# Fewer transfers for values and sketches, another token layout for keys, and a new order of steps in a fused attention and expert kernel

## The chip, the cores and the metric

The kernel runs on one core of a Trainium2 chip. A core has a matrix engine (TensorE, "PE" in the profile; its weight loads are listed as "PEld"), a vector engine (VectorE, "DVE"), a scalar engine (ScalarE, "ACT"), GpSimd ("POOL") and a sync engine (SyncE, "SP") that issues most transfers. Sixteen DMA engines move data between device memory and the on-chip SBUF; matrix products land in PSUM, in banks of 512 float32 columns. Each engine runs its own instructions in order and waits for others through semaphores. The metric is the time of one execution on the device in microseconds; lower is better.

## The reference

A polynomial-sketch attention feeds an expert layer with a rational activation. Shapes: 4 batches, 4 heads, 1088 tokens, 32 features per head, sketches of size 8; the expert layer has 4352 tokens, width 128 and 2048 hidden units.

```python
def phi(x):
    a = np.einsum('rd,bhsd->bhsr', S1, x)
    b = np.einsum('rd,bhsd->bhsr', S2, x)
    return np.einsum('bhsi,bhsj->bhsij', a, b).reshape(*x.shape[:-1], r * r)
q_p, k_p = (phi(q), phi(k))
kv = np.einsum('bhsf,bhsd->bhfd', k_p, v)
z = np.sum(k_p, axis=2)
num = np.einsum('bhsf,bhfd->bhsd', q_p, kv)
den = np.einsum('bhsf,bhf->bhs', q_p, z)[..., None] + 1e-06
x = num / den                       # heads side by side: 4352 x 128
h = x @ w_in
P = a[0] + a[1] * h + a[2] * h**2 + a[3] * h**3
Q = 1.0 + np.abs(b[0]) * np.abs(h) + np.abs(b[1]) * h**2
out = (P / (Q + 1e-06)) @ w_out
```

The sum over tokens in kv and z does not depend on the order in which a batch's key tokens are laid out, as long as keys and values agree.

## The kernel before

The program is one list of steps, ORDER, written out by hand; a loop at the end of the kernel walks it and emits each step's instructions. There is no scheduler: the place of a step in the list sets its place in the queue of every engine that it uses, and only semaphores hold an instruction back. A step's name has its kind, its batch or unit, and its part; a last ".a" or ".d" puts it on ScalarE or VectorE.

- K steps, batch by batch: T0 to T2 transpose the keys on VectorE (L266, L270), s0 and s1 sketch them on TensorE (L276), c0 and c1 copy one sketch out of PSUM (L242 or L244), f0 and f1 form the 64 features (L288), p0 and p1 multiply them with the values into two PSUM banks (L304), k0 and k1 copy the result into `kvz`.
- Q steps, for a batch's queries in three or four cuts: T transposes (L332), sk sketches, c copies. The first two cuts of batch 0 form the features straight from PSUM (L349, L385). The other eleven, the "spread" ones, write their sketch to a scratch tile `sk_d` in device memory (L365) and read it back (step d), once with each row repeated 8 times (`a_all`, L370) and twice with a block of 8 rows repeated (`b_all`, L373); f multiplies the two (L381). Then p (L392), pl, r and x divide, b transposes back (L420), and kk copies into the ring `xT`.
- The expert layer runs over 22 units (token range, 4 to 16 of the 16 hidden blocks): H is the hidden product in float32 (L471), E moves it to SBUF as bfloat16 on ScalarE, U, W, Y, V, S, G are element-wise passes on VectorE, P is one that either engine can do (L496 on VectorE, L499 on ScalarE), L and X a logarithm and an exponential on ScalarE, Or, Os, Og the three output products (L530), ST and OUT the transpose (L537) and the store (L548).
- F steps fetch a batch's k, v or q; I0 to I3 load `w_in`, the second part of the first queries, the coefficients, and `w_out` (into the tile `ln`); w0 to w5 scale `w_out` into three bfloat16 copies. Zn is n products of a zero tile (L182) that keep TensorE running.

Transfers. Nearly all are issued by SP, in the order of ORDER. The program gives transfers eight completion semaphores in turn, over SP and ACT together; an issue waits until the transfer that last had its semaphore has landed, and everything behind it on SP waits too. The key tile, the query tile and the value tile each have one buffer, so that a fetch also waits for the last reader of the batch before. In the program before, 1088 = 34 x 32 tokens are split so that partition g of a head holds tokens 34g to 34g + 33; a key load is one transfer of 128 rows of 4352 bytes. The values come in four transfers of 32 partitions x 4 heads x 1024 bytes and two of 32 x 4 x 128 bytes. A sketch write is two transfers of 64 rows. The first 512 columns of the first queries are issued by ACT.

Of the kernel before, what the change touches and what calls it, by code (L numbers as in the profile page):

```python
# [30 lines left out]
I0 SS0 K0.T0 K0.T1 Z10 K0.s0 K0.T2 F1.k I1 I2 I3 Q0.0.T K0.s1 K0.c0.a Q0.1.T K0.f0 K0.c1.d Z3 Q0.0.sk K0.f1 K0.p0  # L31
Q0.0.c.d Q0.1.sk Q0.0.f K0.p1 F1.v Q0.1.c.d Q0.1.f K0.k1.a K0.k0.a K1.T0 Z5 Q0.0.p K1.T1 Q0.1.p Q0.2.T Q0.0.pl.a
Q0.0.r K1.T2 Q0.0.x Q0.2.sk Q0.1.pl.a Q0.3.T K1.s0 Q0.2.c.a Q0.1.r Q0.1.x Q0.2.d Q0.0.b K1.c0.d K1.s1 Q0.0.kk.a
K1.f0 H0.0 K1.c1.a K1.f1 w3.a H1.0 AB0 w0.d E0.0 w4.d w5.a U0.0 Q0.3.sk w2.d H2.0 E1.0 W0.0 Q0.3.c.d P0.0.a Y0.0
F1.q Q0.1.b w1.d H2.1 E2.0 U1.0 Q0.1.kk.d L0.0 W1.0 V0.0 K1.p0 E2.1 Y1.0 Q0.3.d K1.p1 Q0.2.f X0.0 U2.0 P1.0.a S0.0
Q0.2.p W2.0 K1.k0.a G0.0 K1.k1.a Or0.0 Q0.2.pl.a Os0.0 L1.0 Q0.2.r Q1.0.T Og0.0 Q0.2.x Q1.0.sk F2.k.v X1.0 Q1.1.T
Q0.2.b Y2.0 Q1.1.sk Q0.2.kk.a Or1.0 Q1.0.c.a H3.0 Q1.2.T L2.0 V1.0 S1.0 H3.1 P2.0.d E3.0 G1.0 X2.0 V2.0 F2.q H3.2
Q0.3.f Q1.0.d E3.1 S2.0 Q0.3.p E3.2 Q1.1.c.d H3.3 G2.0 Q0.3.pl.a P3.0.a K2.T0 H4.0 Q0.3.r Q2.0.T E3.3 Q0.3.x K2.T1
P3.1.a K2.s0 U3.0 H4.1 K2.T2 W3.0 K2.c0.a E4.0 K2.f0 Os2.0 E4.1 Q0.3.b Y3.0 H4.2 Q0.3.kk.a P4.0.a Q1.1.d H4.3
Q1.0.f E4.2 V3.0 L3.0 Q1.0.p Q1.2.sk Q2.0.sk Q1.0.pl.d E4.3 Q1.0.r Q2.1.T Or2.0 Q1.0.x X3.0 U4.0 Os1.0 Q1.0.b  # L40
Og1.0 P4.1.d Og2.0 Q1.0.kk.a L3.1 Q2.2.T H5.0 ST2 F3.q W4.0 OUT2 Q1.2.c.a H5.1 V4.0 X3.1 K2.s1 Q1.2.d E5.0 Q1.1.f
Or3.0 Q2.0.c.a Y4.0 E5.1 H5.2 K2.c1.a P5.0.a K2.f1 Q2.1.sk Q1.1.p L4.0 S3.0 Or3.1 H5.3 Q1.1.pl.a E5.2 Q1.1.r
Q3.0.T X4.0 G3.0 H6.0 E5.3 Or4.0 Q1.1.x E6.0 U5.0 Og3.0 Q2.0.d P5.1.a Q1.2.f H6.1 W5.0 L4.1 V5.0 H6.2 E6.1 X4.1
Q1.2.p Y5.0 H6.3 E6.2 S4.0 Q1.2.pl.a Q2.1.c.a Or4.1 L5.0 Q1.1.b Os3.0 Q1.2.r G4.0 Q1.1.kk.a E6.3 H7.0 X5.0 Q2.1.d
Q2.0.f H7.1 U6.0 P6.0.a Q1.2.x Og4.0 W6.0 E7.0 P6.1.d L5.1 Q1.2.b Y6.0 H7.2 E7.1 Os4.0 X5.1 V6.0 H7.3 E7.2 ST4
Q1.2.kk.a P7.0.d OUT4 L6.0 H8.0 S5.0 K2.p0 E7.3 X6.0 Q2.1.f H8.1 U7.0 P7.1.a Q2.2.sk G5.0 K2.p1 Or5.0 Q2.2.c.a
F3.k.v K2.k0.a W7.0 K2.k1.a Or5.1 L6.1 Os5.0 Q3.1.T V7.0 E8.0 Or6.0 X6.1 Q3.0.sk Y7.0 H8.2 Q2.2.d E8.1 Q2.0.p S6.0
Q3.0.c.a E8.2 H8.3 P8.0.a Q3.2.T G6.0 Q2.1.p E8.3 Og5.0 Q2.0.pl.a L7.0 U8.0 Or6.1 Q2.0.r P8.1.a W8.0 Og6.0 Q2.0.x
K3.T0 X7.0 Y8.0 Q2.0.b K3.s0 Q3.0.d Os6.0 Q2.1.pl.a Q2.0.kk.a L7.1 Q2.2.f Q2.1.r H9.0 K3.T1 K3.c0.a Q2.1.x X7.1
ST6 Q2.2.p K3.f0 OUT6 E9.0 S7.0 H9.1 L8.0 Q3.1.sk V8.0 H9.2 E9.1 X8.0 H9.3 K3.T2 G7.0 E9.2 K3.s1 Q2.2.pl.a  # L50
Q3.1.c.a E9.3 Q3.1.d H10.0 Q2.2.r Q3.0.f K3.c1.a L8.1 U9.0 H10.1 Q2.2.x E10.0 K3.f1 X8.1 Q2.1.b Q2.2.b P9.0.d
Or7.0 W9.0 Or7.1 E10.1 Og7.0 S8.0 P9.1.a Q3.2.sk H10.2 Q2.1.kk.a Y9.0 Q3.2.c.a P10.0.a H10.3 G8.0 Q3.2.d E10.2
Os7.0 L9.0 Q3.1.f H11.0 V9.0 E10.3 Q2.2.kk.a X9.0 H11.1 U10.0 E11.0 K3.p0 P10.1.d L9.1 W10.0 H11.2 V10.0 E11.1
Og8.0 X9.1 Y10.0 H11.3 E11.2 P11.0.a Or8.1 Q3.2.f Or8.0 S9.0 K3.p1 E11.3 L10.0 Os8.0 U11.0 P11.1.d K3.k0.a H12.0
X10.0 ST8 W11.0 OUT8 H12.1 K3.k1.a V11.0 L10.1 Q3.0.p E12.0 Y11.0 Q3.1.p X10.1 H12.2 G9.0 E12.1 Or9.0 Q3.0.pl.a
L11.0 Or9.1 Q3.0.r S10.0 H12.3 E12.2 X11.0 Q3.0.x Q3.2.p G10.0 E12.3 Q3.0.b Os9.0 Q3.2.pl.a L11.1 U12.0 Or10.0
Q3.2.r W12.0 Q3.0.kk.a Or10.1 X11.1 Q3.2.x H13.0 Y12.0 Q3.1.pl.a P12.0.a H13.1 Q3.1.r S11.0 E13.0 Og9.0 L12.0
Q3.1.x H13.2 P12.1.d E13.1 G11.0 X12.0 H13.3 P13.0.d E13.2 Q3.1.b Q3.2.b V12.0 Og10.0 Q3.1.kk.a E13.3 Q3.2.kk.a
H14.0 P13.1.a U13.0 W13.0 H14.1 E14.0 V13.0 L12.1 H14.2 E14.1 Y13.0 Os10.0 X12.1 H14.3 ST10 E14.2 S12.0 OUT10
L13.0 Or11.0 Or11.1 P14.0.d E14.3 H15.0 G12.0 X13.0 H15.1 E15.0 U14.0 L13.1 Og11.0 P14.1.d W14.0 H15.2 E15.1 V14.0  # L60
X13.1 Os11.0 Y14.0 E15.2 H15.3 P15.0.a S13.0 H16.0 E15.3 L14.0 Or12.0 U15.0 Or12.1 P15.1.d E16.0 H16.1 W15.0 X14.0
V15.0 Og12.0 E16.1 L14.1 Os12.0 Y15.0 H16.2 X14.1 ST12 G13.0 OUT12 H16.3 E16.2 L15.0 Or13.0 S14.0 Or13.1 E16.3
H17.0 X15.0 U16.0 H17.1 P16.0.d E17.0 W16.0 L15.1 Or14.1 G14.0 Os13.0 E17.1 X15.1 Y16.0 H18.0 P16.1.a H18.1 S15.0
Og13.0 L16.0 U17.0 G15.0 Or14.0 P17.0.a Os14.0 W17.0 X16.0 Og14.0 V17.0 Y17.0 E18.0 L16.1 ST14 H19.0 V16.0 OUT14
E18.1 Or15.0 X16.1 Or15.1 U18.0 P18.0.d Os15.0 W18.0 L17.0 V18.0 Or16.1 S16.0 Or16.0 X17.0 H19.1 Y18.0 E19.0
Os16.0 S17.0 E19.1 L18.0 H20.0 U19.0 G17.0 Og15.0 W19.0 X18.0 G16.0 H21.0 E20.0 P19.0.a Y19.0 Og16.0 S18.0 L19.0
U20.0 ST16 W20.0 Z5 Or17.0 OUT16 E21.0 V19.0 Os17.0 X19.0 G18.0 Os18.0 Or18.0 Y20.0 P20.0.a S19.0 Og18.0 L20.0
Og17.0 U21.0 V20.0 X20.0 W21.0 ST18 Y21.0 P21.0.a Z4 Or19.0 OUT18 S20.0 Or20.0 G19.0 L21.0 Os19.0 Os20.0 G20.0
X21.0 Og19.0 V21.0 S21.0 Or21.0 Og20.0 G21.0 Os21.0 Og21.0 ST21 OUT21
# [4 lines left out]
def kernel(  # L74
# [45 lines left out]

    def load_k(b):
        t = io.tile([128, S], FP, name="k_sb", bufs=1)
        nc.sync.dma_start(out=t, in_=k[b].rearrange("h (g j) d -> (h g) (j d)", g=32))
        return t
# [6 lines left out]
    def load_v(b):  # L131
        o = v.offset + b * H * S * D
        for m in range(NM):
            nc.sync.dma_start(out=v_sb[m * 32:(m + 1) * 32, :, 0:W],
                              in_=bass.AP(tensor=v.tensor, offset=o + m * W, ap=[[NJ * D, 32], [S * D, H], [1, W]]))
        for jj in range(NL):
            nc.sync.dma_start(out=v_sb[jj * 32:(jj + 1) * 32, :, W:W + D],
                              in_=bass.AP(tensor=v.tensor, offset=o + (NM * NT + jj) * D,
                                          ap=[[NJ * D, 32], [S * D, H], [1, D]]))
# [10 lines left out]
    nc.scalar.dma_start(out=q0[:, 0:512], in_=q0_src[:, 0:512])  # L150
# [102 lines left out]
    class Keys:  # L253
# [7 lines left out]
        def turned(self, part):  # L261
            half = NM * NT * 32
            self.kT = kT
            k_sb = keys_in[self.b]
            if part == 2:
                nc.vector.transpose(out=self.kT[:, half:S], in_=k_sb[:, half:])  # L266
                return
            hT = self.kT[:, 0:half].rearrange("p (t m g) -> p m t g", t=NT, m=NM)
            hk = k_sb[:, 0:half].rearrange("p (m t d) -> p m t d", t=NT, m=NM)
            nc.vector.transpose(out=hT[:, :, part * 4:part * 4 + 4], in_=hk[:, :, part * 4:part * 4 + 4])  # L270
# [50 lines left out]
    class Queries:  # L321
# [12 lines left out]
        def sketches(self):  # L334
            n = self.n
            if self.spread:
                self.sk = bank()[:, 0:n // 2]
                for x in range(2):
                    nc.tensor.matmul(self.sk[x * 2 * H * R:(x + 1) * 2 * H * R],
                                     lhsT=S21.rearrange("p c s h r -> p (c s h r)"),  # L340
                                     rhs=self.qT[:, x * n // 2:(x + 1) * n // 2], start=True, stop=True)
                return
# [17 lines left out]

        def repeated(self):
            n, half = self.n, H * R
            d = dram.tile([half, 2 * QW], FP, name="sk_d")
            for x in range(2):
                nc.sync.dma_start(out=bass.AP(tensor=d.tensor, offset=d.offset + x * n // 2,  # L365
                                              ap=[[n, 2], [2 * QW, half], [1, n // 2]]),
                                  in_=self.c[x * 2 * half:(x + 1) * 2 * half, :n // 2])
# [9 lines left out]
        def features(self):  # L377
            n = self.n
            if self.spread:
                self.q_p = self.a[:, :2 * n].rearrange("p (c n) -> p c n", c=2)  # L380
                nc.vector.tensor_mul(out=self.q_p, in0=self.q_p,  # L381
                                     in1=self.bb[:, :2 * n].rearrange("p (c n) -> p c n", c=2))
                return
            self.q_p = self.a
            nc.vector.tensor_mul(out=self.a[:, :, :n], in0=self.both[:, :, n:2 * n], in1=self.a[:, :, :n])  # L385

# [166 lines left out]
    def fetch(b, *what):  # L553
        if "k" in what:
            keys_in[b] = load_k(b)
        if "v" in what:
            load_v(b)
# [65 lines left out]
```

## Time and profile before

| What | Value |
|---|---|
| median of 3 runs | 279.95 us (279.64 to 280.8) |
| the profiled execution, its own time | 277.88 us |
| its span, first to last instruction | 275.7 us |
| DVE L491, L503, L516, L520, 22 each | 39.5, 39.5, 39.5, 39.4 us |
| PE L471 | 125.2 us in 320 records |
| ACT L477, L508, L512 | 69.2, 66.0, 66.0 us |
| SP waits for sk_d to land before reading it (L370) | 42.9 us in 13 waits |
| DMA | 20.12 MB, 29020 packets, mean 73 GB/s |

The busy time of an engine is the union of its instructions; matmuls are pipelined, so a busy TensorE is not one at its peak. A row of a table of windows gives start:end, length, then busy time and count for PE, PEld, DVE, ACT and POOL, then the granted TensorE clock as a share of full speed, the mean busy share of the 16 DMA engines, and GB/s. A row of the chain of waits gives start, length and what the chain passed through. A row of the longest waits gives the waiting engine, its tile and line, what ended the wait, the total in us, the number of waits and the longest. Idle time of SP costs nothing in itself.

### The profile page before, as it was taken

To read this page: it belongs to the slowest core of one execution; us is meant where nothing else is said; L and a number is where in the kernel's file an instruction comes from. 1 tells how busy PE (TensorE), PEld (TensorE's weight loads), DVE (VectorE), ACT (ScalarE), POOL (GpSimd) and SP (SyncE) were. 2 spreads that over 40 slices of the span, in tenths; PEclk is the share of its full clock that TensorE was granted. 3 is DMA by queue.
4 is the path that set the end of the run, shared out by engine and by line. 5 is a ranking of instruction groups with operands and counts; after the bars stand their busy time and mean duration, and the time that the engine had idled before them with its cause. 6 is when DMAs were issued, how large, how long until landed. Compare 5 with 4: busy or idle time off the path is not lost.

```text
span 275.7 us, 3737 instructions
## 1 busy us (share of the span) xinstructions
PE 265.0 (96%) x1416; PEld 153.9 (56%) x1432; DVE 254.8 (92%) x245; ACT 243.2 (88%) x223; POOL 2.9 (1%) x24
## 2 busy tenths in 40 slices
PE   6999999969999999999999999999999999999994
PEld 1688865546645445565544456544444457456683
DVE  1769997987999999999999989999999999999994
ACT  1016999977999999999999999999999999999991
POOL 4000000000000000000000000000000000000000
PEclk9689999989999999999999999999999999999999
DMA  6971578325222325234032102000020020020021
GB/s 190 304 211 46 156 181 157 108 86 147 96 85 75 110 38 160 79 104 106 13 109 78 42 1 40 1 0 0 0 40 0 0 38 2 0 38 0 14 42 23
DMA packets 29020, 20.12 MB, mean 73 GB/s; under 512 B 20812, under 2 KB 24268, under 8 KB 29004
## 3 DMA queue, kind: packets, MB, share of 16 engines
q1 hardware_dynamic: 28172, 19.56, 27.8%
q10 hardware_dynamic: 832, 0.34, 0.5%
q8 instruction: 11, 0.18, 0.3%
q14 instruction: 5, 0.04, 0.0%
HBM read 16.68 MB, written 3.21 MB: 72 GB/s over the span
## 4 chain that ended last, share of the span: by engine, by line
PE 60%; DVE 16%; DMA 9%; ACT 8%; issue 5%; SPq 1%; DVEq 0%
PE h_ps L471 23%; PE out_ps L530 21%; PE att_ps L392 4%; PE att_ps L304 4%; DVE g L520 3%; ACT r L512 3%; DMA v_sb<-in_v_dram 3%; DVE w L491 3%; ACT ln L508 3%; DVE g L503 2%; ACT hh L477 2%; DMA sk_d<-sk_sb 2%; DMA b_all<-sk_d 2%; DMA k_sb<-in_k_dram 2%; PE att_ps L276 2%
## 5 line engine op out<-in xcount | busy, mean ns | idle before, releaser
L471 PE MATMUL h_ps<-xT,w_in_sb 128*128 128x512 f32 (+1 forms) x320 | 125.2, 532 | 0.6 <-ACT hh L477 0.6
L471 PEld LDWEIGHTS h_ps<-xT,w_in_sb 128*128 128x128 f32 x320 | 59.2, 190 | 44.5 <-issue 35.7
L530 PEld LDWEIGHTS <-w_out 128*128 128x128 bf16 x480 | 47.2, 100 | 46.3 <-issue 10.5
L477 ACT CAST hh<-h_ps 128x1024 bf16<-128x1024 f32 x68 | 69.2, 1022 | 1.4 <-PE h_ps L471 1.1
L508 ACT ACTIVATE ln<-w 128x2048 f32<-128x2048 bf16 (+1 forms) x36 | 66.0, 1833 | 0.4 <-DVE w L491 0.2
L512 ACT ACTIVATE r<-ln 128x2048 bf16<-128x2048 f32 (+1 forms) x36 | 66.0, 1834 | 0.3
L499 ACT ACTIVATE g<-hh,a_sb 128x2048 bf16<-128x2048 bf16 (+1 forms) x22 | 43.0, 1953 | 0.0
L516 DVE TENSOR_TENSOR s<-hh,r 128x4096 bf16<-128x4096 bf16 (+2 forms) x22 | 39.5, 1794 | 0.7 <-ACT r L512 0.7
L503 DVE TENSOR_TENSOR g<-g,hh 128x4096 bf16<-128x4096 bf16 (+2 forms) x22 | 39.5, 1795 | 0.0
L491 DVE TENSOR_TENSOR w<-w,u 128x4096 bf16<-128x4096 bf16 (+2 forms) x22 | 39.5, 1794 | 0.0
L520 DVE TENSOR_TENSOR g<-g,s 128x4096 bf16<-128x4096 bf16 (+2 forms) x22 | 39.4, 1793 | 0.0
L530 PE MATMUL out_ps<-r,w_out 128*128 128x512 bf16 (+1 forms) x152 | 33.5, 353 | 0.4
L530 PE MATMUL out_ps<-s,w_out 128*128 128x512 bf16 (+1 forms) x158 | 32.9, 350 | 0.2 <-issue 0.2
L530 PE MATMUL out_ps<-g,w_out 128*128 128x512 bf16 (+1 forms) x156 | 32.5, 346 | 0.2
L486 DVE TENSOR_SCALAR w<-u,b_abs 128x4096 bf16<-128x4096 bf16 (+2 forms) x22 | 24.0, 1091 | 0.0
L392 PEld LDWEIGHTS att_ps<-kvz,a_all 128*128 128x128 f32 x148 | 17.9, 192 | 7.1 <-DVE a_all L381 3.4
L481 DVE TENSOR_SCALAR u<-hh 128x4096 uint16<-128x4096 uint16 (+2 forms) x22 | 21.5, 975 | 0.1
L392 PE MATMUL att_ps<-kvz,a_all 128*128 128x66 f32 x148 | 18.0, 273 | 2.3 <-DVE a_all L381 2.3
L304 PEld LDWEIGHTS att_ps<-v_sb,k_p 128*64 128x64 f32 (+1 forms) x288 | 10.1, 147 | 3.5 <-issue 2.6
L242 ACT COPY kvz<-att_ps 64x33 f32<-64x33 f32 x16 | 2.9, 181 | 9.6 <-PE att_ps L304 9.4
L304 PE MATMUL att_ps<-v_sb,k_p 128*64 128x64 f32 (+1 forms) x288 | 11.3, 235 | 0.0
L496 DVE TENSOR_SCALAR g<-hh,a_sb 128x2048 bf16<-128x2048 bf16 x14 | 11.3, 804 | 0.0
(58 smaller groups left out, 132.5 us busy)
## 6 DMA issues: line engine op xcount, KB each, us to landing
k_sb<-in_k_dram SPq DMA_DIRECT2D x4, 544.0 KB
a_all<-sk_d SPq DMA_DIRECT2D x6, 352.0 KB
b_all<-sk_d SPq DMA_DIRECT2D x12, 176.0 KB
v_sb<-in_v_dram SPq DMA_DIRECT2D x16, 128.0 KB
q_sb<-in_q_dram SPq DMA_DIRECT2D x3, 544.0 KB
a_all<-sk_d SPq DMA_DIRECT2D x3, 384.0 KB
b_all<-sk_d SPq DMA_DIRECT2D x6, 192.0 KB
w_in_sb<-in_moe_w_in_dram SPq DMA_DIRECT2D x2, 512.0 KB
```

The costliest lines, as they stand in the source:

```text
L304: nc.tensor.matmul(self.kv[h // 2][p0:p0 + 64, 0:64].rearrange("p (n d) -> p n d", d=D), lhsT=self.k_p[part][:sl, t - t0, h].rearrange("p ...
L392: nc.tensor.matmul(self.nd[:self.tl, o:o + 2 * KW], lhsT=self.q_p[:, c, self.at[t]:self.at[t] + self.tl], rhs=kvz[self.b % 2][:, c, :], st ...
L471: nc.tensor.matmul(t[:, (x - part * m) * tl:(x - part * m + 1) * tl], lhsT=w_in_sb[:, (f0 + x) * 128:(f0 + x + 1) * 128], rhs=xT[:, p:p + ...
L477: nc.scalar.copy(out=at(i, "hh", c, ce), in_=live[i]["h", part][:, :ce - c])
L491: nc.vector.tensor_mul(out=at(i, "w", *c), in0=at(i, "w", *c), in1=at(i, "u", *c))
L499: nc.scalar.activation(out=at(i, "g", *c), in_=at(i, "hh", *c), func=ACT.Identity, scale=a3, bias=a2)
L503: nc.vector.tensor_mul(out=at(i, "g", *c), in0=at(i, "g", *c), in1=at(i, "hh", *c))
L508: nc.scalar.activation(out=t[:, :ce - c], in_=at(i, "w", c, ce), func=ACT.Ln, bias=1.0 + 1e-6)
L512: nc.scalar.activation(out=at(i, "r", c, ce), in_=live[i]["ln", k][:, :ce - c], func=ACT.Exp, scale=-1.0)
L516: nc.vector.tensor_mul(out=at(i, "s", *c), in0=at(i, "hh", *c), in1=at(i, "r", *c))
L520: nc.vector.tensor_mul(out=at(i, "g", *c), in0=at(i, "g", *c), in1=at(i, "s", *c))
L530: nc.tensor.matmul(outs[t0][:, :tl], lhsT=w_sb[y][:, f0 + x, :], rhs=at(i, "rsg"[y], x * tl, (x + 1) * tl), start=first and j == 0, stop=l ...
```

## The change

What it does:

- Key tokens are laid out so that partition g of a head holds tokens 32g to 32g + 31 (the first 1024) and then two of the last 64. A key load becomes two transfers, 1024 and 64 columns wide, whose source pattern is 4 heads x 32 rows x columns. The transposes T0 to T2 write `kT` in the matching order: T0 and T1 with a step of 4 elements, T2 with a step of 2.
- The values of a batch come in two transfers, 128 partitions x 4 heads x 1024 bytes and 64 x 4 x 128 bytes.
- A spread sketch is made by four matmuls of 32 stationary columns where there were two of 64, so that the rows of the PSUM tile come in four blocks; it is written to `sk_d` by one transfer whose destination has an outer count of 4.
- The step d is split into dw (write) and dr (the reads), placed apart in ORDER.
- The first query piece is issued by SP, behind the first keys, and not by ACT.
- ORDER is new throughout: groups of zero products 12, 5, 4, 1, 1 early and 2, 3, 3, 1 at the end (10, 3, 5 and 5, 4 before); fetches of keys and queries stand earlier; some copies, parts of w and P steps change between ScalarE and VectorE (nine P steps to VectorE, seven away).

```diff
 ORDER = """
-I0 SS0 K0.T0 K0.T1 Z10 K0.s0 K0.T2 F1.k I1 I2 I3 Q0.0.T K0.s1 K0.c0.a Q0.1.T K0.f0 K0.c1.d Z3 Q0.0.sk K0.f1 K0.p0
-Q0.0.c.d Q0.1.sk Q0.0.f K0.p1 F1.v Q0.1.c.d Q0.1.f K0.k1.a K0.k0.a K1.T0 Z5 Q0.0.p K1.T1 Q0.1.p Q0.2.T Q0.0.pl.a
...
+I0 SS0 K0.T0 K0.T1 Z12 K0.s0 K0.T2 F1.k I1 I2 I3 Q0.0.T K0.s1 K0.c0.a Q0.1.T K0.f0 K0.c1.d Z5 Q0.0.sk K0.f1 K0.p0
+Q0.0.c.d Q0.1.sk Q0.0.f K0.p1 F1.v Q0.1.c.a Q0.1.f K0.k0.a K0.k1.d K1.T0 Z4 Q0.0.p Q0.2.T Q0.1.p K1.T1 Q0.0.pl.a
+Q0.0.r K1.T2 Q0.2.sk Q0.0.x Q0.1.pl.a Q0.1.r Z1 K1.s0 Q0.3.T Q0.1.x F1.q Q0.2.c.d Q0.0.b K1.c0.d Z1 K1.s1 Q0.2.dw
+Q0.0.kk.a K1.f0 H0.0 K1.c1.a w4.a w3.d K1.f1 AB0 w0.a H1.0 F2.k w5.d E0.0 Q1.0.T w2.a Q0.3.sk U0.0 Q0.2.dr Q1.0.sk
+P0.0.d H2.0 W0.0 E1.0 Q1.1.T Q0.3.c.d w1.a Y0.0 Q0.3.dw K1.p0 Q1.2.T P1.0.a U1.0 F2.q K1.p1 V0.0 Q1.0.c.a W1.0
+E2.0 Q1.0.dw V1.0 Q0.1.b F2.v H2.1 Y1.0 L0.0 K1.k0.d Q0.1.kk.a K1.k1.d X0.0 Q0.2.f Q0.3.dr Q1.1.sk K2.T0 Q1.2.sk
+E2.1 Q0.2.p S0.0 Q1.1.c.a K2.T1 L1.0 Q1.1.dw K2.s0 U2.0 Q0.2.pl.a Q1.2.c.a K2.T2 Q0.2.r F3.k Or0.0 W2.0 P2.0.a
+K2.s1 Q0.2.x G0.0 Q1.2.dw Q0.2.b Q2.0.T Os0.0 Q0.2.kk.a Og0.0 Y2.0 K2.c0.a X1.0 H3.0 Q2.1.T K2.c1.a L2.0 Q0.3.f
+Q1.0.dr H3.1 S1.0 K2.f0 E3.0 Or1.0 Q1.1.dr G1.0 X2.0 Q2.0.sk K2.f1 H3.2 E3.1 Q2.2.T Q0.3.p S2.0 F3.q Q2.0.c.a E3.2
+Q2.0.dw V2.0 H3.3 Q0.3.pl.a P3.0.a Q0.3.r Q1.0.f H4.0 Q0.3.x Q1.2.dr E3.3 G2.0 P3.1.a Q2.1.sk U3.0 Q1.0.p Q1.1.f
...
@@ def load_k
-        nc.sync.dma_start(out=t, in_=k[b].rearrange("h (g j) d -> (h g) (j d)", g=32))
+        o = k.offset + b * H * S * D
+        for c, n in ((0, NM * W), (NM * W, NL * D)):
+            nc.sync.dma_start(out=t[:, c:c + n],
+                              in_=bass.AP(tensor=k.tensor, offset=o + c * 32, ap=[[S * D, H], [n, 32], [1, n]]))
@@ def load_v
-        for m in range(NM):
-            nc.sync.dma_start(out=v_sb[m * 32:(m + 1) * 32, :, 0:W],
-                              in_=bass.AP(tensor=v.tensor, offset=o + m * W, ap=[[NJ * D, 32], [S * D, H], [1, W]]))
-        for jj in range(NL):
-            nc.sync.dma_start(out=v_sb[jj * 32:(jj + 1) * 32, :, W:W + D],
-                              in_=bass.AP(tensor=v.tensor, offset=o + (NM * NT + jj) * D,
-                                          ap=[[NJ * D, 32], [S * D, H], [1, D]]))
+        nc.sync.dma_start(out=v_sb[:, :, 0:W], in_=bass.AP(tensor=v.tensor, offset=o, ap=[[W, 128], [S * D, H], [1, W]]))
+        nc.sync.dma_start(out=v_sb[0:NL * 32, :, W:W + D],
+                          in_=bass.AP(tensor=v.tensor, offset=o + SM * D, ap=[[D, NL * 32], [S * D, H], [1, D]]))
@@ the first query piece
-    nc.scalar.dma_start(out=q0[:, 0:512], in_=q0_src[:, 0:512])
+    nc.sync.dma_start(out=q0[:, 0:512], in_=q0_src[:, 0:512])
@@ Keys.turned
-                nc.vector.transpose(out=self.kT[:, half:S], in_=k_sb[:, half:])
+                nc.vector.transpose(out=self.kT[:, half:S].rearrange("p (g j) -> p j g", j=NL),
+                                    in_=k_sb[:, half:].rearrange("p (j d) -> p j d", j=NL))
-            hT = self.kT[:, 0:half].rearrange("p (t m g) -> p m t g", t=NT, m=NM)
+            hT = self.kT[:, 0:half].rearrange("p (t g m) -> p m t g", t=NT, m=NM)
@@ Queries.sketches
-                    nc.tensor.matmul(self.sk[x * 2 * H * R:(x + 1) * 2 * H * R],
-                                     lhsT=S21.rearrange("p c s h r -> p (c s h r)"),
-                                     rhs=self.qT[:, x * n // 2:(x + 1) * n // 2], start=True, stop=True)
+                    for c in range(2):
+                        nc.tensor.matmul(self.sk[(2 * c + x) * H * R:(2 * c + x + 1) * H * R],
+                                         lhsT=S21[:, c].rearrange("p s h r -> p (s h r)"),
+                                         rhs=self.qT[:, x * n // 2:(x + 1) * n // 2], start=True, stop=True)
@@ Queries.repeated, now written and repeated
-            for x in range(2):
-                nc.sync.dma_start(out=bass.AP(tensor=d.tensor, offset=d.offset + x * n // 2,
-                                              ap=[[n, 2], [2 * QW, half], [1, n // 2]]),
-                                  in_=self.c[x * 2 * half:(x + 1) * 2 * half, :n // 2])
+            nc.sync.dma_start(out=bass.AP(tensor=d.tensor, offset=d.offset,
+                                          ap=[[n // 2, 4], [2 * QW, half], [1, n // 2]]),
+                              in_=self.c[:, :n // 2])
@@ Queries.features
-                self.q_p = self.a[:, :2 * n].rearrange("p (c n) -> p c n", c=2)
-                nc.vector.tensor_mul(out=self.q_p, in0=self.q_p,
-                                     in1=self.bb[:, :2 * n].rearrange("p (c n) -> p c n", c=2))
+                nc.vector.tensor_mul(out=self.a[:, :2 * n], in0=self.a[:, :2 * n], in1=self.bb[:, :2 * n])
```

## The prediction

> **What bounds the kernel now.** I read the busy times first, then a table of windows, then the longest waits and the chain.
>
> ```profile
> PE 265.0 (96%) x1416; PEld 153.9 (56%) x1432; DVE 254.8 (92%) x245; ACT 243.2 (88%) x223; POOL 2.9 (1%) x24
> ```
>
> Three engines are nearly full, so no single one is "the" bound; what counts is where VectorE (DVE) is not busy, 275.7 - 254.8 = 20.9 us in all. The windows (start:end, length, busy time of each engine, granted clock, DMA share, GB/s) say where:
>
> ```profile
> 0.00:10.00 10.00, 7.04 (x29) 4.00 (x30) 4.22 (x11) 1.55 (x2) 2.92 (x24) 0.94 0.77 223
> 10.00:20.00 10.00, 9.84 (x105) 6.84 (x105) 6.17 (x10) 0.73 (x4) 0.00 (x0) 0.72 0.81 246
> ...
> 40.00:50.00 10.00, 10.00 (x39) 5.65 (x38) 7.98 (x13) 9.79 (x9) 0.00 (x0) 1.00 0.76 145
> 50.00:60.00 10.00, 7.66 (x40) 4.58 (x40) 8.72 (x7) 9.68 (x10) 0.00 (x0) 1.00 0.32 88
> 60.00:70.00 10.00, 9.95 (x53) 6.44 (x51) 8.57 (x13) 6.64 (x9) 0.00 (x0) 0.83 0.51 146
> 70.00:170.00 100.00, 99.58 (x530) 53.31 (x534) 98.61 (x76) 98.92 (x92) 0.00 (x0) 1.00 0.28 78
> 170.00:270.00 100.00, 99.01 (x432) 55.52 (x440) 99.96 (x83) 99.29 (x76) 0.00 (x0) 1.00 0.08 12
> ```
>
> From 70 to 270 us VectorE idles 1.4 us in 200: nothing is to be won or hidden there, and whatever is late at 70 us is late at the end. Its idle time is 9.6 us before 20 us, 5.9 us from 20 to 70 us (five windows, the two left out have 0.9 and 0.2), 4 us at the end. The waits name the pieces:
>
> ```profile
> DVE out_sb L537 <- PE out_ps L530: 3.0, 3, 1.4
> DVE kT L270 <- DMA k_sb<-in_k_dram: 3.0, 1, 3.0
> DVE qT L332 <- DMA q_sb<-in_q_dram: 1.8, 1, 1.8
> ...
> DVE a_all L381 <- DMA b_all<-sk_d: 1.3, 1, 1.3
> ```
>
> and the chain of waits ties the middle two together:
>
> ```profile
> 1.48 5.08 DMA k_sb<-in_k_dram
> ...
> 10.16 1.28 PE out_ps L182 x3
> 11.44 2.01 PE h_ps L349 x8
> ...
> 36.74 7.70 DMA v_sb<-in_v_dram
> 44.47 5.68 DMA sk_d<-sk_sb
> ...
> 51.49 5.46 DMA b_all<-sk_d
> ```
>
> At the start all waits for the first keys (landed at 6.56 us). At 36.7 us SP issues keys, six value transfers and queries in a row; the sketch write behind them goes out at 43.87 us, as the key load (issued at 36.20) gives its semaphore back. TensorE then idles 2.3 us, the granted clock drops (0.83 in 60 to 70 us), and the output transpose at 65 us waits 1.4 us: 1.8 + 1.3 + 1.4 = 4.5 us is what better DMA timing could win.
>
> **The change, part by part.**
>
> *Sketch writes and value loads.* One write replaces two: SP's two issues took 1.1 us (rows "1.10 L365"), one takes about 0.55. Eleven writes, and 6 value transfers to 2 (2.7 us of issue to about 0.9), four times. In this stretch they free SP and the eight semaphores that transfers share in turn, and are what moves the 43.87 us issue forward. I credit q_sb 1.8 and b_all 1.3: **-3.1 us**; the 1.4 at 65 us I leave, since TensorE will idle elsewhere.
>
> *Key loads, the part that I think decides.* The data are the same, but the source of the large piece now has 4 outer rows (heads) over 32, where it had 128 rows. What the outer count does is seen in three windows that each hold one kind of transfer (sketch writes, outer count 2; the reads of b_all, 8; a key load, 128):
>
> ```profile
> 111.40:113.40 2.00, 2.00 (x10) 0.82 (x9) 2.00 (x1) 2.00 (x2) 0.00 (x0) 1.00 0.14 42
> 117.90:118.70 0.80, 0.80 (x8) 0.71 (x8) 0.70 (x2) 0.80 (x3) 0.00 (x0) 1.00 0.61 193
> 104.00:105.50 1.50, 1.50 (x4) 0.45 (x3) 1.50 (x3) 1.50 (x2) 0.00 (x0) 1.00 0.85 313
> ```
>
> The shares of 16 engines are 0.14, 0.61 and 0.85: about 2, 8 to 10, and nearly all. The semaphore updates per transfer agree (3, 9 and 16 in the trace). So four outer rows should mean 4 engines. One engine moves 313 / (16 x 0.85) = 23 GB/s here; a 4096-byte packet of the weight load took 160 ns, which is 25.6. The 512 KB are then 5.1 to 5.7 us on four engines; I take 5.4. The first key packet left at 3.5 us and landing takes about 0.6 more: keys at 9.5 us instead of 6.56. Nothing covers it, for the three transposes of the keys are first on VectorE: **+2.9 us**. Were all 16 engines used it would be 0. The bounds are 0 and 3.2.
>
> The Trainium skill, page "DMA: Bandwidth & Descriptors", section "Why a DMA increments its semaphore by 16 and not by 1", says that the number of engines is the largest one up to 16 that divides the outermost counts of both sides; for 4 against 128 that is 4. No load with 4 rows is in this trace; by that rule the start costs the 2.9 above, by the bytes alone it would cost nothing.
>
> *First query piece.* It moves from ACT's queue to SP's, behind both key pieces. On the four shared engines it follows them (0.7 us): about 10.6 us, when the three key transposes (1.4 us from 9.5) are done at 10.9. No further cost; 0 to 0.5.
>
> *Zero products.* 27 become 32. The first 12 end at 1.19 + 12 x 0.44 = 6.5 us, ahead of the keys: free. The second group, 5 for 3, stands right ahead of the first L349, on the chain, where three took 1.28 us at a granted clock of 0.50: 2 x 0.43 = **+0.9 us**. The other groups stand in waits or at the end: 0, at most 0.4.
>
> *What queues behind the four engines.* This is the wait that I expect in place of the removed one. SP's queue on those engines, in its new order: keys 0, q0 (0.7), values (2.2), w_in (2.6), keys 1 to 21 us, the second half of q0, w_out (3 to 4), values 1, queries 1, the write of Q0.2, then keys 2 (5.7 with its small piece) and only then the reads of Q0.2, which land near 38 us. VectorE starts K1.T0 at 17.95 + 2.9 + 0.9, about 21.6, and has 13.4 us of work (group means, in the new order) and 1.6 us of small waits before that step: ready near 36.5. Stall 0 to 1.5. Farther on keys 3 are issued before the write of Q1.2 and the reads of Q1.0: their 5.7 us push these reads to about 56.3, where VectorE is ready near 52.6. Stall 0 to 3.7. ScalarE and TensorE can't run ahead far: hidden products wait for free banks. Of 5.2 I take **+3.8 us**, since slack in one arrival eats into a sum over so many.
>
> *Four sketch blocks.* 4 matmuls of 32 columns for 2 of 64. Two of 64 run 0.45 us (chain, 4 records) with both halves starting 6 ns apart, so halves overlap. If four quarters overlap as well the cost is 0; if only pairs do, 0.45 us each, and 9 of the 11 stand where TensorE is on the chain (60 to 164 us): 4.1. I take 0, as each quarter streams the same columns.
>
> The Trainium skill, page "TensorEngine Tiling (Array Packing)", section "Theoretical Speedup", gives up to 4x for a side of at most 32, which would be the 0; the trace shows only the twofold case.
>
> *Key transposes with a stride.* 8 of 0.62 us now write every fourth element. Nothing in the trace writes so; 0, at most as much again, 5.0 in all. I take 0: the contiguous qT transposes have the same cost per element.
>
> *Work that changes engine.* Nine P steps go to VectorE and seven away, copies and w parts both ways; by group means VectorE gets 0.4 us less, ScalarE 0.5 less: **-0.4**. Flattening the product of L381 changes no size.
>
> **Sum.** 2.9 + 0.9 - 3.1 + 3.8 - 0.4 = +4.1 us. The profiled execution took 277.88 us (span 275.7), 2.1 under the median of 279.95, so a median near **284.0 us** (own range 281 to 287.5).
>
> **Rivals.**
> - *Faster: the early stalls go and none comes.* Decided where the reads of Q0.2 and Q1.0 land before VectorE is ready (36.5 and 52.6 us). Then 2.9 + 0.9 - 4.5 - 0.4 = -1.1: 278.9. For it: fewer transfers and earlier issues. Against: 5.7 us of keys ahead of each read on the same engines.
> - *Faster: key loads keep all engines.* 0.9 - 4.5 - 0.4 = -4.0: 276.0. Against: the three shares above.
> - *Slower still:* quarters don't overlap (+4.1, 288.1) or strided transposes cost double (+5.0, 289). For the first: TensorE is on the chain for 100 us.
>
> **How the numbers follow.** Forecast 0.55; early stalls gone 0.18; 16 engines 0.10; slower still 0.17. The measurement tells 0.5% (1.4 us) from no change, so the bounds are 278.55 and 281.35. The forecast gives 0.50 slower, 0.05 same; the first rival 0.08 faster, 0.08 same, 0.02 slower; the second is faster, the third slower. Together 0.18 faster, 0.13 same, 0.69 slower. The range 277.0 to 289.0 leaves out most of the 16-engine case and the far end of the last.
>
> **What would show it.** The first transpose of keys after 9 us instead of 6.58, with a DMA share near 0.25 while a key load runs alone; a sketch write at a share near 0.25 too and 1 us shorter; VectorE waits on b_all before the products of Q0.2 or Q1.0; the records of L339 in groups of four starting within some 20 ns. Keys before 7.5 us, or no b_all wait, would prove the forecast wrong.

## The result, and the profile after

The changed kernel took **292.12 us** (median of 4 runs, 291.08 to 295.86) where the kernel before, on the same chip, took 279.79 (278.22 to 280.80). The ratio is **1.044**, 95% interval 1.038 to 1.050: slower by 12.3 us, three times the +4.1 us of the forecast and above its range (277 to 289). Some executions of a kernel are disturbed and slower; medians count them, ratios and intervals leave them out, and the profiled execution of the changed kernel is one of them (295.86 us, span 293.9; the four others had spans of 289.2 to 290.9), so places and durations are read from it below, not its sum.

The waits of VectorE after (total, times, longest):

```profile
DVE kT L273 <- DMA k_sb<-in_k_dram: 11.8, 2, 11.1
DVE a_all L386 <- DMA b_all<-sk_d: 8.7, 4, 4.2
```

These were 3.0 and 1.3 us before. The wait on q_sb (1.8) is gone, as forecast; what replaced it is far larger. The windows after:

```profile
0.00:10.00 10.00, 4.27 (x12) 1.48 (x12) 0.92 (x5) 1.28 (x1) 2.92 (x24) 0.88 0.65 118
10.00:20.00 10.00, 3.99 (x19) 3.99 (x20) 3.90 (x6) 0.27 (x1) 0.00 (x0) 0.50 0.61 134
20.00:30.00 10.00, 10.00 (x109) 6.56 (x107) 4.95 (x8) 1.01 (x4) 0.00 (x0) 0.76 0.85 165
...
40.00:50.00 10.00, 6.70 (x106) 5.28 (x104) 5.77 (x15) 6.90 (x10) 0.00 (x0) 0.93 0.70 178
50.00:60.00 10.00, 10.00 (x48) 8.89 (x48) 8.17 (x15) 5.66 (x10) 0.00 (x0) 0.56 0.39 129
60.00:70.00 10.00, 10.00 (x43) 4.99 (x41) 6.19 (x8) 9.31 (x10) 0.00 (x0) 1.00 0.86 216
...
170.00:270.00 100.00, 100.00 (x432) 52.64 (x431) 99.60 (x71) 99.58 (x79) 0.00 (x0) 1.00 0.08 11
```

VectorE (third busy figure) works 4.8 us of the first 20, where it worked 10.4 before, and 5.0 to 8.2 of 10 in four of the five windows from 20 to 70 us. TensorE idles, and the granted clock (third figure from the end) falls to 0.50 there and to 0.56 once more. After 170 us the engines are as full as before. The chain up to 70 us (start, length):

```profile
1.49 13.36 DMA k_sb<-in_k_dram
14.87 1.99 DVE kT L273 x2
16.94 12.35 DMA k_sb<-in_k_dram
33.33 4.32 DMA sk_d<-sk_sb
38.90 9.88 DMA b_all<-sk_d
52.86 11.55 DMA k_sb<-in_k_dram
64.43 8.97 DMA b_all<-sk_d
```

Key loads and reads of sketches (b_all) follow one another. Two key loads in a row, 13.4 and 12.4 us from issue to landing where the forecast had 8.0 for the first, stand ahead of the first expert product. Its place is in the timeline of that line (count, durations in ns, first and last start), before and then after:

```profile
L471 PE MATMUL h_ps<-xT,w_in_sb x320: 379/592/697, 23.5 to 257.4; 128*128 128x512 f32 x112, 128*128 128x256 f32 x48
```

```profile
L480 PE MATMUL h_ps<-xT,w_in_sb x320: 379/592/697, 34.9 to 276.1; 128*128 128x512 f32 x112, 128*128 128x256 f32 x48
```

The experts start 11.4 us late; nothing later gives that back.

### The profile page after: what moved, and what is told of

It is laid out like the page before. It is cut to its first block, busy times and chain, and to the rows that moved or that the text cites. A ratio compares the mean times of both kernels' runs of the same rounds, so it can differ in the third digit from the quotient of the medians.

```text
span 293.9 us, 3813 instructions
## 1 busy us (share of the span) xinstructions
PE 271.1 (92%) x1481; PEld 157.5 (54%) x1481; DVE 257.2 (87%) x249; ACT 242.1 (82%) x219; POOL 2.9 (1%) x24
## 4 chain that ended last, share of the span: by engine, by line
DVE 33%; PE 23%; DMA 23%; ACT 13%; issue 6%; SPq 1%; DVEq 0%
DMA k_sb<-in_k_dram 13%; PE h_ps L480 11%; DMA b_all<-sk_d 9%; PE out_ps L539 8%; DVE g L529 6%; DVE s L525 5%; DVE w L500 4%; ACT hh L486 4%; DVE g L512 4%; ACT ln L517 4%; ACT r L521 4%; DVE w L495 3%; DVE u L490 3%; DVE kT L273 2%; DVE g L505 2%
## 5 line engine op out<-in xcount | busy, mean ns | idle before, releaser
L508 ACT ACTIVATE g<-hh,a_sb 128x2048 bf16<-128x2048 bf16 (+1 forms) x20 | 40.4, 2018 | 0.1
L539 PE MATMUL out_ps<-r,w_out 128*128 128x512 bf16 (+1 forms) x160 | 34.6, 351 | 0.2 <-DVE out_sb L546 0.2
L539 PE MATMUL out_ps<-g,w_out 128*128 128x512 bf16 (+1 forms) x160 | 33.2, 349 | 0.1
L401 PEld LDWEIGHTS att_ps<-kvz,a_all 128*128 128x128 f32 x148 | 19.3, 203 | 8.3 <-DVE a_all L386 5.1
L401 PE MATMUL att_ps<-kvz,a_all 128*128 128x66 f32 x148 | 19.3, 284 | 4.4 <-DVE a_all L386 4.4
L273 DVE STREAM_TRANSPOSE kT<-k_sb 128x512 f32<-128x512 f32 x8 | 8.6, 1088 | 11.8 <-DMA k_sb<-in_k_dram 11.8
L386 DVE TENSOR_TENSOR a_all<-a_all,b_all 128x704 f32<-128x704 f32 (+2 forms) x11 | 9.7, 880 | 8.7 <-DMA b_all<-sk_d 8.7
L279 PE MATMUL h_ps<-S,kT 128*128 128x64 f32 x18 | 4.1, 424 | 10.6 <-DVE kT L273 10.6
```

What stands on the lines that cost most here:

```text
L401: nc.tensor.matmul(self.nd[:self.tl, o:o + 2 * KW], lhsT=self.group(t, c), rhs=kvz[self.b % 2][:, c, :], start=True, stop=True)
L508: nc.scalar.activation(out=at(i, "g", *c), in_=at(i, "hh", *c), func=ACT.Identity, scale=a3, bias=a2)
L539: nc.tensor.matmul(outs[t0][:, :tl], lhsT=w_sb[y][:, f0 + x, :], rhs=at(i, "rsg"[y], x * tl, (x + 1) * tl), start=first and j == 0, stop=l ...
```

## The experiments

Medians of different calls come from different chips (before: 279.42, 278.24, 279.67 and 278.77 us), so ratios to the kernel before on the same chip are what is compared. "First keys" is the start of the first transpose, 6.58 us before and 14.87 after.

### Which part of the change costs the time

**Only the key load's form, put into the kernel before.** The value addresses follow the keys' token step; six value transfers, contiguous transposes and the old order stay.

```
-        nc.sync.dma_start(out=t, in_=k[b].rearrange("h (g j) d -> (h g) (j d)", g=32))
+        for c, n in ((0, NM * W), (NM * W, NL * D)):
+            nc.sync.dma_start(out=t[:, c:c + n],
+                              in_=bass.AP(tensor=k.tensor, offset=o + c * 32, ap=[[S * D, H], [n, 32], [1, n]]))
...
```

> The kernel before with only the key loads of the change: two transfers with a source pattern of 4 heads x 32 rows; the six value transfers keep their form and their place, with the token step that matches (32 tokens per partition). Transposes, sketches and order are those of before. Theory (four engines move the keys, at half their speed when other loads run beside them): first key transpose near 14 us as in the changed kernel, 6.6 before, no stall added by the transposes; time 288 to 292. Rival 1 (the new order and its zero products cost the time): within 2 us of before, 278 to 282. Rival 2 (the keys are slow because the values come in one large transfer beside them): first key transpose near 9 us, time 283 to 285.

Measured: 295.09 us, ratio 1.056 (1.052 to 1.060), above the theory's 288 to 292, with the first keys at 14.2 us, as it said. One of its waits:

```profile
DVE kT L273 <- DMA k_sb<-in_k_dram: 14.3, 3, 10.6
```

The key load alone makes the kernel slower than the whole change does. Neither the new order nor the large value transfer is needed for it.

**The change, with the large key piece as one transfer for each head.** The bytes, places and order are the same; each transfer's source has 32 rows instead of 4. The 32 KB piece stays one transfer of 4 x 32 rows.

```
+        for h in range(H):
+            nc.sync.dma_start(out=t[h * 32:(h + 1) * 32, 0:NM * W],
+                              in_=bass.AP(tensor=k.tensor, offset=o + h * S * D, ap=[[NM * W, 32], [1, NM * W]]))
...
```

> The changed kernel with the large key piece split by head into four transfers of 32 rows each (outer count 32 on both sides); all else as changed, the 32 KB piece still 4 x 32 rows. Theory (four engines): keys land near 7 us again, the b_all waits of 8.7 us mostly go; what stays is the strided transposes (3.2 us) and two zero products: 280 to 284. Rival (order and zero products): stays at 288 to 292 though the keys are early.

Measured: 278.11 us, ratio 0.989 (0.985 to 0.994), faster than the theory's 280 to 284. First keys at 6.0 us, each of the first batch's four transfers landed 2.6 to 2.8 us after its issue (those of the second batch, beside w_in, took 8.3 to 8.5), and the two waits shrank:

```profile
DVE a_all L389 <- DMA b_all<-sk_d: 3.6, 5, 1.0
DVE kT L276 <- DMA k_sb<-in_k_dram: 3.2, 2, 2.4
```

The ratio falls from 1.044 to 0.989, and to 0.993 in a repeat below: 14 to 15 of the 292 us hang on the outer row count of one access pattern. In the trace the four-row load updates its semaphore 5 times, each per-head transfer 16 times.

**The change, with key loads, value loads and key transposes of before.** Order, zero products, q0 on SP, sketch blocks and the single write stay.

> The changed kernel with key loads, value loads and key transposes put back to those of before; sketches, split write and reads, order and zero products as changed. Theory (four engines, and 0.4 us more per strided transpose): 276 to 280, some 3 us under a_kh. Rival (order): 286 to 292. If the order is a gain by itself it is under 279.

Measured: 275.14 us, ratio 0.984 (0.980 to 0.987), slightly under the theory's 276 to 280. Without the key and value forms the change is a gain of 1.6%; the next two runs show where it comes from.

**Only the sketches, put into the kernel before:** four row blocks and one write.

> The kernel before with only four sketch blocks and one write per sketch (outer count 4). Theory (four quarters overlap on TensorE, a write uses 4 engines where two writes used 2): each write lands some 1 us sooner, the wait on b_all at 57 us shrinks from 1.3 us; 278 to 280. Rival (TensorE pays 0.45 us per sketch): 281 to 284.

Measured: 273.66 us, ratio **0.979** (0.974 to 0.983), more than was expected. The windows from 40 to 70 us:

```profile
40.00:50.00 10.00, 10.00 (x39) 5.66 (x38) 9.69 (x16) 9.81 (x9) 0.00 (x0) 1.00 0.71 155
50.00:60.00 10.00, 10.00 (x69) 6.58 (x68) 9.93 (x11) 9.87 (x10) 0.00 (x0) 1.00 0.36 115
60.00:70.00 10.00, 9.95 (x57) 6.09 (x56) 9.95 (x10) 10.00 (x12) 0.00 (x0) 1.00 0.40 113
```

VectorE had 7.98, 8.72 and 8.57 there, and TensorE 7.66 in the middle one. The whole stall that the prediction described is gone: the write that was issued at 43.87 us goes out at 41.91, and the reads behind it land at 53.15 instead of 56.95. TensorE no longer idles, the clock stays at 1.00, and the output transpose at 65 us doesn't wait either. VectorE works 4.3 us more in these 30 us, most of what was won.

**Order, zero products and q0's queue alone**; all other forms as before.

> The new order, the five more zero products and the first query piece on SP's queue, with key loads, value loads, transposes, sketch products and sketch writes as before. Theory, what the runs so far sum to: the single write is worth 5.8 us in either order, and the new order costs 1.4 us: 275.1 + 5.8 = 280.9 us (279.5 to 282.5). Rival, the new order doesn't need the single write, and its price lies elsewhere: 275 to 278.

Measured: 281.61 us, ratio 1.012 (1.006 to 1.019), as the sum of the other runs had it. The new order is no gain by itself: in its trace VectorE waits 5.8 us for b_all, 1.3 before. With the single write the new and the old order come to 275.1 and 273.7 us.

### Why a key load took 13 us and not 8

**The other loads held back until the first keys are there.** A 4 KB write from the keys to a scratch tensor, on SP right behind them, makes SP wait.

```
     k0 = load_k(0)
+    seen = dram.tile([128, 8], FP, name="seen", bufs=1)
+    nc.sync.dma_start(out=seen, in_=k0[:, 0:8])
```

> The changed kernel, with a 4 KB write from the keys of batch 0 to a scratch tensor issued on SP right behind the key load, so that q0, values and w_in are issued only when the keys have landed. It tells what made the first key load 13.4 us long. Theory, the other loads on the same four engines: alone, the 4096-byte packets take about 160 ns instead of 316 (median), so 32 on each engine take 5.1 us, the keys land near 9.5 us and the first transpose starts there instead of at 14.87; the time is 292.1 - 5.4 = 286.7 us (285 to 290, as values and w_in come later). Rival, a source of four long rows is slow by itself: packets of 300 ns stay, the first transpose is at 13.5 to 15 us, and the time 292 to 296.

The keys came at 10.96 us, between the two theories but with the packets of the first: alone, they take 159 ns (median). Only the first ones are slow (seven of the first nine took 0.3 to 1.7 us, and from 3 to 5 us the load moved 14 GB/s), which is about the 1.4 us that the estimate lacked. The windows of that kernel show four engines and nothing else:

```profile
6.00:8.00 2.00, 0.05 (x1) 0.00 (x0) 0.00 (x0) 0.00 (x0) 0.00 (x0) 1.00 0.26 92
8.00:10.00 2.00, 0.00 (x0) 0.00 (x0) 0.00 (x0) 0.00 (x0) 0.00 (x0) 0.72 0.25 99
```

92 and 99 GB/s at a quarter share are 22 to 25 GB/s for each engine, the figure that the forecast used. Beside the other loads it looks different. First the kernel before, then the changed one:

```profile
8.00:10.00 2.00, 2.00 (x16) 2.00 (x15) 1.88 (x4) 0.27 (x1) 0.00 (x0) 0.70 0.95 337
10.00:12.00 2.00, 2.00 (x8) 0.80 (x8) 1.78 (x3) 0.00 (x0) 0.00 (x0) 0.50 0.97 313
```

```profile
8.00:10.00 2.00, 0.00 (x0) 0.00 (x0) 0.00 (x0) 0.00 (x0) 0.00 (x0) 0.50 1.21 179
10.00:12.00 2.00, 0.00 (x0) 0.00 (x0) 0.00 (x0) 0.00 (x0) 0.00 (x0) 0.50 1.01 172
```

The share adds up the time of packets, so it can pass 1. It is 0.95 and more in both, but the second moves about half as much: q0, values and w_in are on their way beside the keys, and the 4096-byte packets, those of the keys and of w_in, take 307 ns (median from 2.5 to 30 us) where w_in's took 163 before. So the load is long for two reasons: four engines, and packets that take twice as long beside other traffic. The second isn't the four-row load's alone: in the per-head kernel, with all but 32 KB of a batch's keys on 16 engines, these packets take 252 ns from 8 to 17 us.

The time was 294.26 us, ratio 1.060 (1.052 to 1.067): rather a loss against 1.044, and the expected 286.7 was wrong. The 3.9 us that the first keys won were lost to the second ones, which took 15.1 us where they had taken 12.4. W_in, landed at 20.2 and 22.4 us, now ran beside these; that it is the cause wasn't tested:

```profile
1.48 9.46 DMA k_sb<-in_k_dram
14.24 15.12 DMA k_sb<-in_k_dram
```

The second keys landed at 29.36 us, against 29.30 as changed.

### In which batch

**Batch 0 alone split by head; batches 1 to 3 alone; batches 0 and 1.** The edit is that of the per-head load under `if b == 0`, `if b > 0` and `if b < 2`.

> The changed kernel, with the large key piece of batch 0 alone split into one transfer for each head (32 source rows, 16 engines); the other three batches load on four engines as changed. Splitting all four batches gave 278.1 us against 292.1. Theory, the delays add up: the first transpose comes at 6.0 to 6.6 us instead of 14.87, and the 8.3 us between are won in full, 283.8 us (282 to 286); the other 5.7 us stay, in the VectorE waits on k_sb and b_all after 30 us. Rival, the later loads are only covered because the start is late: VectorE waits longer later, and the time is 287 to 291.

> The complement: batch 0 loads its keys on four engines as changed, batches 1 to 3 with one transfer for each head. Theory, the delays add up: the first transpose stays near 14.9 us, the later waits on k_sb and b_all fall from some 10 us to 4, and the time is 278.1 + 8.3 = 286.4 us (285 to 288). Rival, the late start covers the later loads, so that they cost little of their own: 289 to 292.

> The changed kernel, with the key loads of batches 0 and 1 split into one transfer for each head, and batches 2 and 3 on four engines as changed. In the traces so far the first expert product starts at 34.9 us as changed, 29.0 with batch 0 split, 32.4 with batches 1 to 3 split, and 23.6 with all split. Theory, the two loads in a row ahead of the experts are the cost: the experts start at 23 to 25 us, and the time is 278 to 281 us, ratio to before 0.99 to 1.005. Rival, the loads of batches 2 and 3 have a price of their own through the reads of b_all behind them: 282 to 286 us, ratio 1.01 to 1.03, with VectorE waits on b_all of 5 us or more.

| Split | ratio (95%) | first keys | second keys turned | first expert product |
|---|---|---|---|---|
| none (as changed) | 1.044 (1.038 to 1.050) | 14.87 us | 29.32 us | 34.9 us |
| batch 0 | 1.035 (1.029 to 1.042) | 5.98 | 21.11 | 29.0 |
| batches 1 to 3 | 1.025 (1.019 to 1.031) | 14.31 | 26.89 | 32.4 |
| batches 0 and 1 | 1.020 (1.013 to 1.028) | 6.01 | 18.93 | 24.5 |
| all | 0.989 (0.985 to 0.994) | 6.04 | 18.06 | 23.6 |

In the first row's kernel the loads of batches 0 and 1 stand one behind the other. With batch 0 split the first keys come 8.9 us earlier, but only 0.9% are won, within the intervals: VectorE waits for the second keys instead, 5.5 us in one wait. That is the rival's range (287.43 us), while batches 1 to 3 came out just under their theory's (284.65 us). With batches 0 and 1 split the experts start within a microsecond of where they do with all split, and 3% are still missing; there the rival was right (284.84 us, and 7.4 us of waits on b_all). The chain of that run says where:

```profile
28.54 8.98 DMA b_all<-sk_d
...
49.92 10.49 DMA b_all<-sk_d
```

These reads stand behind the keys of batches 2 and 3. With all four loads split the same two take 3.6 and 7.0 us instead of 9.0 and 10.5, and VectorE's waits on b_all are 3.6 us instead of 7.4. In the kernel before such reads land in 3.9 to 5.5 us, so the second is slow in the changed kernel even without the four-row loads. Each four-row load has a price of its own, and a part of it shows only when the load ahead of it is mended.

### The strided transposes

**Transposes written contiguously, with the values in five transfers to match; then contiguous transposes alone, beside an unchanged per-head kernel on the same chip.**

```
-            hT = self.kT[:, 0:half].rearrange("p (t g m) -> p m t g", t=NT, m=NM)
+            hT = self.kT[:, 0:half].rearrange("p (t m g) -> p m t g", t=NT, m=NM)
...
```

> The per-head key load for all batches (278.1 us), with the transposes of the large piece written contiguously again (the column order of before) and the large value transfer in four parts of 32 partitions, so that values and keys match. Theory, the strided write costs 0.4 us for each of 8 transposes (1084 against 690 ns): 278.1 - 3.2 = 274.9 us (273.9 to 276.5), which is what the kernel with the key and value forms of before took (275.1). Rival, the transposes are hidden, or the merged value transfer was worth as much: 277 to 280.

> The per-head key load with the transposes of the large piece written contiguously and nothing else changed: loads, queues and order stay those of the kernel that took 278.1 us. The keys then stand in another token order than the values (the output is not the reference's). It gives the strided write alone, which the run with five value transfers mixed with their issue. Theory, 8 x 0.4 us are on VectorE's path: 274.9 us, ratio to before 0.973 to 0.983. Rival, other waits take the 3.2 us: ratio 0.986 to 0.994, 277 to 279 us.

> The per-head key load for all batches once more, without any change, beside the run with contiguous transposes on the same chip: 278.1 us, ratio to before 0.985 to 0.994.

In the second of these kernels keys and values no longer match; it shows times only. The stride does cost VectorE time. The groups of the key transposes, before and then after (busy us and mean ns behind the bar):

```profile
L270 DVE STREAM_TRANSPOSE kT<-k_sb 128x512 f32<-128x512 f32 x8 | 5.4, 688 | 3.0 <-DMA k_sb<-in_k_dram 3.0
```

```profile
L273 DVE STREAM_TRANSPOSE kT<-k_sb 128x512 f32<-128x512 f32 x8 | 8.6, 1088 | 11.8 <-DMA k_sb<-in_k_dram 11.8
```

0.40 us each, 3.2 us in all. But the time doesn't show it. With five value transfers: 278.83 us, ratio 1.004 (1.001 to 1.008), not faster than with the strided form. Contiguous transposes alone: 278.64 us, ratio 0.990 (0.985 to 0.995), beside 276.80 us and 0.993 (0.988 to 0.997) for the unchanged one. The rival held both times. In the first, three more value transfers for each batch stand on SP's queue, and the ratio is 1.2 to 1.5% higher than that of the strided form; that they are the cause wasn't separated.

### Tries at a faster kernel

Three variants of the kernel with the sketches alone (0.979) aim at the start, where VectorE waits 3.3 us for the first keys.

```
-    s_raw = [spread_s(e, i, t) for i, (e, t) in enumerate(((nc.scalar, S1), (nc.sync, S2)))]
-    k0 = load_k(0)
+    s_raw = [spread_s(nc.sync, i, t) for i, t in enumerate((S1, S2))]
+    k0 = load_k(0, nc.scalar)
...
```

This is the second; the first issues S2 on ACT's queue instead, and the third adds to the first the order `K0.T0 K0.T1 SS0`.

> A try at a faster kernel: the kernel before with four sketch blocks and one sketch write (273.7 us), and the load of S2 issued on ACT's queue instead of on SP's ahead of the keys. Theory: the first key load is issued at 0.73 us instead of 1.48, all waits for it until 6.58 us, so 0.75 us are won: 272.9 us, first transpose at 5.8 to 6.0. Rival, S2 or the first query piece, which now queues behind it on ACT, comes late: 273.5 to 275, first transpose at 6.4 or later.

> A try at a faster kernel: before with four sketch blocks and one write (273.7 us), the first keys issued on ACT's queue at 0.73 us, S1 and S2 on SP's queue ahead of the values. In the run with S2 on ACT the keys landed at 4.6 us instead of 6.6, but S2 only at 6.4 behind the values. Theory: keys and S2 are both there by 5.0 us, the first transpose starts at 4.7 to 5.3 and 1.5 us are won: 272.2 us, ratio 0.970 to 0.978. Rival, the first query piece, now behind the keys on ACT's queue, or the chip's state at the start takes it back: 273 to 274.5.

> The same aim by the order: S2 on ACT's queue as in the run that took 273.0 us, and the first two key transposes ahead of the sketch weights on VectorE, so that the keys (landed at 4.6 us) are turned while S2 (6.4 us) is still under way. Theory: transposes at 4.7 and 5.4 us, weights at 6.4, the first key products at about 7.2 instead of 7.7: 0.5 us won, 272.5 to 273.2. Rival, the weights' chain over two engines is as long as the transposes were: 273 to 274.5, first products at 7.5 or later.

Measured: 273.04 us and 0.978 (0.972 to 0.984); 271.77 and 0.976 (0.971 to 0.981); 273.60 and 0.982 (0.976 to 0.988). None can be told from the 0.979 that they start from. In the first two the wait moved from the keys to S2 (the first transpose stayed at 6.8 and 6.7 us, where the theories had 5.8 to 6.0 and 4.7 to 5.3). In the third it came at 4.5 us and the experts started at 21.7 instead of 23.9, but the time didn't follow. Its trace has VectorE waits of 3.6 us on q_sb and 3.6 on the output products (none and 1.6 in the kernel it starts from); whether the gain was lost there wasn't tested.

## Why the prediction went as it did

The direction was right and so was its mechanism: four outer rows are four engines, and what is queued behind such a load waits. The size was wrong, in the key loads above all. In ratios the measured parts close: 5.2 to 5.5% for the key loads, 1.2% for order and zero products and -2.1% for the sketches make 4.3 to 4.6%, and 4.4% were measured. That leaves the merged value loads and the strided transposes near nothing, within some 1%.

- **Key loads, +2.9 us.** This step failed, though its engine count held. Its duration, 5.4 us for 512 KB, took the rate of an engine in a window with one kind of transfer, and the same sum noted q0, values and w_in on SP's queue without charging them to the keys. The load alone took 9.5 us from issue to landing where the estimate had 8.0; beside the others 13.4. The first transpose was 8.3 us late where the term's bounds were 0 and 3.2. The second keys, forecast to land by 21 us, landed at 29.3, and the experts started 11.4 us late. The rule of the Trainium skill, page "DMA: Bandwidth & Descriptors", section "Why a DMA increments its semaphore by 16 and not by 1", that the largest common divisor of the outer counts up to 16 is the number of engines, agrees with this trace: a share of 0.25 and 5 semaphore updates for 4 rows, as 3 for 2 rows and 9 for 8 before, and 16 for 32. It gives the count, not the rate beside other loads.
- **Stalls behind the four engines, +3.8 us.** Place right, size off by the same rate. The forecast priced a key load at 5.7 us ahead of the reads; from issue to landing it took 11.6 to 12.4, and the reads 9 to 11. VectorE waited 8.7 us for b_all: 4.2 before the product of Q0.2 (forecast 0 to 1.5), 3.6 before that of Q1.0 (0 to 3.7), and 0.9 in two later places. Not all of it is the four engines': 3.6 us of such waits stay with the per-head loads. The two terms, +6.7 in the sum, are 14 to 15 us by the per-head runs.
- **Sketch writes, -3.1 us with the value loads.** Too small: the sketches alone won 5.8 us. The prediction left the 1.4 us at 65 us standing, since "TensorE will idle elsewhere"; once the write went out 2 us earlier it didn't idle.
- **First query piece, 0.** Late, but no cost of its own: it landed at 15.78 us where the sum had 10.6, behind the keys (14.85), and no VectorE wait names it.
- **Zero products, +0.9 us.** On the chain as forecast: five stand for 2.13 us in the kernel with batch 0 alone on four engines, where three stood for 1.28. Their share of the time wasn't measured alone.

```profile
15.44 4.11 PE h_ps L283 x18
19.55 2.13 PE out_ps L188 x5
21.68 1.06 PE h_ps L357 x8
```

- **Four sketch blocks, 0.** Right. The quarters start within some 20 ns of each other, and a sketch's products of 144 columns, now 8 records, take 0.45 us where 4 records took 0.47. (The price of the rival, 4.1 us, was too high: it counted nine of the eleven sketches from 60 us on, and seven start after 59 us.)

```profile
30.86 0.45 PE L343 MATMUL att_ps<-qT,S 128*32 128x144 f32 x8
```

- **Strided transposes, 0.** Right for the time and wrong for its reason: the instruction became 58% longer, from a mean of 688 ns (the sum took 0.62 us), which nothing excluded. VectorE presumably had waits to put it in.
- **Work that changes engine, -0.4 us.** Not tested alone. With the order and the zero products it costs 1.2% (0.6 to 1.9%); the sum had +0.5 us for these, so the order has a price that it lacks.
- **The rivals.** Sixteen engines: refuted by the share of 0.25. No new stall: refuted by the waits. What came true, the forecast's mechanism at twice its price, was not among them, as the bounds of the key term came from loads that had their engines to themselves.

## What to carry to other kernels

Look at the outer row count of each side of a transfer before its bytes: one piece with 4 outer rows in each batch cost 14 to 15 us of 292, and the same bytes in four pieces of 32 rows gave them back. Price a load by a window in which it shares its engines with what will really run beside it, and give the rate a bound from the slowest such packets. When one of several queued loads is mended, expect the wait to move to the next: two of four mended here won less than half.

## What the runs showed of the hardware

- Full shares hide a lost rate: at a share of 1.0 to 1.2 the engines moved 172 to 197 GB/s from 6 to 14 us in the changed kernel, 306 to 343 in five of six windows from 4 to 16 us before. The per-head kernel has both, 321, 212, 328 and 210 from 6 to 14 us, so the four-row load isn't the only cause. Which resource the packets contend for was not tested.
- A 128x512 transpose on VectorE took 1088 ns writing every fourth element, 688 in contiguous runs of 32.
- A sketch write with 4 outer rows landed 3.0 us after its issue in quiet stretches, as long as one with 2 rows and half the bytes; two of the latter took 4.1 us from the first issue to the last landing. One write for two won 2.1% (1.7 to 2.6%), 5.8 us over eleven sketches. Whether the issue saved or the two engines more counted wasn't separated.
